# Batch 0's last transform stage moved into the end of the hand-ordered loop, with pools on both sides of SBUF

## The chip, the cores and the metric

The kernel runs on one NeuronCore of a Trainium2 chip. The metric is device time in microseconds (us). Three runs of the kernel before took 1730.43, 1730.86 and 1733.43 us; the median is 1730.86. A profile describes one more execution, instruction by instruction. Its engines are PE (TensorE's matmuls), PEld (TensorE's weight loads), ACT (ScalarE), DVE (VectorE), POOL (GpSimd) and SP (SyncE, which issues every DMA of this kernel; SPq in the rows).

## The reference

Two layers follow each other, on 8 batches of 3136 positions and 256 channels:

```python
X = np.fft.rfft(x, axis=1)
Yr = Xr @ w_r - Xi @ w_i + b_r
Yi = Xr @ w_i + Xi @ w_r + b_i
Yr = np.sign(Yr) * np.maximum(np.abs(Yr) - lam, 0.0)      # and Yi
y = np.fft.irfft(Yr + 1j * Yi, n=3136, axis=1)

h = np.maximum(y @ w_in, 0.0)                             # 256 -> 1024
conv_out = three-tap convolution of h along the positions, per channel
gate = 1.0 / (1.0 + np.exp(-conv_out))
out = (h * gate) @ w_out                                  # 1024 -> 256
```

So the first half is a spectral layer: a real Fourier transform along the positions, a complex 256 x 256 mix of the channels, a soft threshold, and the inverse transform. The second half is a gated feed-forward network (FFN).

## The kernel before

**Transforms as matmuls.** 3136 = 56 x 56, so each transform is two steps of small matmuls with tables of cosines and sines. Stage 1 (`stage1_pe`, L269) does the first step of the forward transform and stores its result in DRAM (`sc1`). Stage 2 (`stage2`, L312) does the second step, on a group of four frequencies `u`, and splits the result in a high and a low part. `mix` (L340) multiplies by the channel weights in three products of those parts. `shrink` (L349 to L355) is the soft threshold: two Relu on ScalarE into `r` and `q`, and a subtraction on GpSimd. Stage 3 (`stage3_pe`, L363) is the first step of the inverse transform; `stage3_out` copies its result to `z1` on ScalarE (L369) and stores it in DRAM (`sc2`) by two DMAs (L372, L378; four where the group is the first of a batch). Stage 4 (`stage4`, L495) is the last step: it loads `z2` from `sc2` (L489), multiplies by `i2`, and moves the result into `y`, which holds a whole batch in SBUF as a high part `yh` (ScalarE, L501) and a low part `yl` (VectorE, L502).

**The transform loop.** 8 batches of 7 groups make 56 items, `n_it = 56`. The loop at L427 runs 60 iterations and works as a pipeline: iteration `it` does stage 3 of item `it - 4`, stage 1 of an item further ahead, stage 2 of item `it`, `shrink` of item `it - 2`, `third` (the sum's high and low part) of item `it`, and `mix` of item `it - 1`. Stage 1 runs about ten items ahead, and is through by iteration 46. The last four iterations, 56 to 59, only drain the pipeline. In `background`, from iteration 3, VectorE prepares the FFN's weights in small steps between the others.

**What sets the order.** The loop stands in `with tc.manual_schedule()`. Inside it, each engine issues its instructions in the order in which the program text emits them, SyncE's DMAs too. Everything else is placed by a planner that goes by its own costs and by priorities, and it may put later instructions between those of the loop. Stage 4 of batch 0 stands behind the loop, with a raised priority (`HP = 500`), and so is placed by the planner. Stage 4 of the other batches is called from the FFN loop, three pieces per chunk, for the batch after the one in work.

**Stage 4 in pieces.** A batch has 28 values of `j`, in `NPC = 7` pieces of `JG = 4`. A piece loads one `z2` of 112 x 4 x 256 numbers (448 KB), does 8 matmul calls (16 in the profile) into one PSUM tile of two banks, and moves it out in two parts (three in piece 0), both channel halves together. `zio` holds three `z2` tiles.

**The FFN.** For each chunk of two times 448 positions and each of eight blocks of 128 hidden channels, `up` (L520) multiplies, applies Relu (L522), the three taps (L525 to L529), the sigmoid (L530) and the gate (L531), and splits the result (L534, L535); `down` (L548) multiplies by `w_out`, four blocks later. `y` is double: `y_a` for even and `y_b` for odd batches. The first `up` needs all of batch 0's `y`.

**Memory.** Every pool of the transform part is released when the loop ends (`ab`); the FFN's pools, `zio`, `y_a` and `y_b` among them, then take their place. A tile waits for those earlier tiles only whose bytes it takes.

Of the kernel before, what the change touches and what calls it, by code (L numbers as in the profile page):

```python
# [9 lines left out]
F32 = mybir.dt.float32  # L10
F32R = mybir.dt.float32r
I32 = mybir.dt.int32
AF = mybir.ActivationFunctionType
ALU = mybir.AluOpType
# [3 lines left out]
B, S, D, FF = 8, 3136, 256, 1024  # L18
R = 56
U = 28  # L20
SL = 57
SP = 64
H = 28
LAM = 0.01
UG = 4
NG = U // UG
JC = 4
P = 128
NT = D // P
NF = FF // P  # L30
CH = 448


def _tables():
# [90 lines left out]
def spectral_ffn_kernel(ctx: ExitStack, tc: tile.TileContext, x, w_r, w_i, b_r, b_i,  # L125
                        w_in, conv_w, w_out, fwd1, fwd2, inv1, inv2, out):
    nc = tc.nc
    K1, K2 = 2 * R, 2 * SP
# [3 lines left out]
    sc2 = [dram.tile([H, 4, U, D], F32, name=f"sc2_{b}") for b in range(B)]  # L132
# [4 lines left out]
    i2 = cst.tile([K1, 240], F32, name="i2")[:, 0:2 * K1].rearrange("p (a m) -> p a m", a=2)  # L137
# [4 lines left out]
    mlam, warm = small[:, 0:1], small[:, 1:2]  # L142


    with ExitStack() as ab:
        stg = ab.enter_context(tc.tile_pool(name="stg", bufs=1))
        wbp = ab.enter_context(tc.tile_pool(name="wbp", bufs=2))
        s1p = ab.enter_context(tc.tile_pool(name="s1p", bufs=2))
        c1 = ab.enter_context(tc.tile_pool(name="c1", bufs=1))
        a2p = ab.enter_context(tc.tile_pool(name="a2p", bufs=3))  # L150
        cmx = ab.enter_context(tc.tile_pool(name="cmx", bufs=1))
# [1 line left out]
        psx = ab.enter_context(tc.tile_pool(name="psx", bufs=6, space=PSUM))  # L153
        psa = ab.enter_context(tc.tile_pool(name="psa", bufs=1, space=PSUM))

        f1 = c1.tile([P, P], F32, name="f1")[:, 0:SP]
        t2 = c1.tile([K1, U, K2], F32, name="t2")
        bias = cmx.tile([P, 2, D], F32, name="bias")
        cmx.tile([P, 96], F32, name="pad")
# [161 lines left out]
        def third(xs):  # L321
            fh, fl, d = xs
            nc.scalar.copy(fh[:, :, 2], d)
            nc.gpsimd.tensor_tensor(fl[:, :, 2], d, fh[:, :, 2].bitcast(F32), op=ALU.subtract)  # L324
            return fh, fl

        def mix(xs):


            fh, fl = xs  # L330
            ps = {c: psx.tile([K2, UG // 2, D], F32, name=f"ps_mx{c}", tag="bank") for c in (2, 0, 1)}
            for c in (2, 0, 1):
                q = (1, 2, 0)[c]
                for k in range(UG // 2):
                    mm = []
                    for t in range(NT):
                        a = [f[:, t, c, 2 * k:2 * k + 2, :] for f in (fh, fl)]
                        mm += [(a[0], wmix_hi[:, t, q, :]), (a[0], wmix_lo[:, t, q, :]), (a[1], wmix_hi[:, t, q, :])]
                    for n, (lt, rh) in enumerate(mm):
                        nc.tensor.matmul(ps[c][:, k, :], lt, rh, start=(n == 0), stop=(n == len(mm) - 1))  # L340
            p1 = wk.tile([K2, 2, UG // 2, D], F32, name="p1")
            v = wk.tile([K2, 2, UG // 2, D], F32, name="v")
            for c in range(2):
                nc.vector.tensor_tensor(p1[:, c], ps[2], bias[:, c:c + 1, :].to_broadcast([K2, UG // 2, D]), op=ALU.add)
            for c in range(2):
                nc.vector.tensor_tensor(v[:, c], ps[c], p1[:, c], op=ALU.add)
            return v

        def shrink(v):  # L349
            r = wk.tile([K2, 2, UG // 2, D], F32, name="r", bufs=3)  # L350
            q = wk.tile([K2, 2, UG // 2, D], F32, name="q", bufs=1)
            nc.scalar.activation(r, v, AF.Relu, bias=mlam)
            nc.scalar.activation(q, v, AF.Relu, bias=mlam, scale=-1.0)  # L353
            nc.gpsimd.tensor_tensor(r, r, q, op=ALU.subtract)  # L354
            return r  # L355

        def stage3_pe(g, r):
# [28 lines left out]
        n_it = len(items)  # L386
        WP0, LAST = 3, n_it - 6
        a2s = {}
        p1 = NG
# [30 lines left out]
        def fetch(n):  # L420
            nonlocal nx
            while len(xq) < n and nx < n_it:
                xq.append(load_x(s1p, *items[nx], bufs=XRB)[0])
                nx += 1

        with tc.manual_schedule():
            for it in range(n_it + LAG):  # L427
                if it + 2 < n_it:
                    a2s[it + 2], _ = load_a2(*items[it + 2])
                if it < NG:  # L430
                    load_inv1(it)
                    if it + 1 < NG:
                        load_t2(it + 1)
                fetch(XRB)
                if it >= LAG:
                    g3 = items[it - LAG]
                    ps3 = stage3_pe(g3[1], ss.pop(it - LAG))
                if p1 < n_it:
                    ps1 = stage1_pe(xq.pop(0))
                if it >= LAG:  # L440
                    stage3_out(*g3, ps3)
                if WP0 <= it < n_it:
                    next(background, None)
                if p1 < n_it:
                    stage1_out(*items[p1], ps1)
                    p1 += 1
                if WP0 <= it < n_it:
                    for _ in range(2):
                        next(background, None)
                if it < n_it:  # L450
                    xs[it] = stage2(items[it][1], a2s.pop(it))
                if 0 <= it - 2 < n_it:
                    ss[it - 2] = shrink(vs.pop(it - 2))
                if it < n_it:
                    xs[it] = third(xs[it])
                if 0 <= it - 1 < n_it:
                    vs[it - 1] = mix(xs.pop(it - 1))
                if p1 < n_it and p1 < min(it + AHEAD, NG + 2 + it + it // 2):
                    fetch(1)
                    ps1 = stage1_pe(xq.pop(0))  # L460
                    stage1_out(*items[p1], ps1)
                    p1 += 1


    def pool(name, bufs=1, **kw):
        return ctx.enter_context(tc.tile_pool(name=name, bufs=bufs, reuse_waits="tile", **kw))

    zio, y_a = pool("zio", 3), pool("y_a")
    wk, hp, io, y_b = pool("cwk"), pool("chp", 3), pool("cio"), pool("y_b")
    wk.tile([P, 24], F32, name="pad", bufs=1)  # L470
    SW = 3168
    hp.tile([P, 8], F32, name="pad", bufs=1)
    psh, pso = pool("psh", 2, space=PSUM), pool("pso", space=PSUM)

    JG = 4
    NPC = H // JG

    def new_y(b):
        y = [(y_a, y_b)[b % 2].tile([P, NT, SW], F32R, name=nm) for nm in ("yh", "yl")]
        for q in y:  # L480
            qf = q.bitcast(F32)
            nc.vector.memset(qf[:, :, 0:1], 0.0)
            nc.vector.memset(qf[:, :, S + 1:S + 2], 0.0)
        return y

    def stage4(b, jg, y):

        z2 = zio.tile([K1, JG, D], F32, name="z2")
        nc.sync.dma_start(z2, sc2[b].rearrange("j q u e -> (q u) j e")[:, jg * JG:(jg + 1) * JG, :])  # L489
        ps = psh.tile([P, NT, 512], F32, name="ps_s4", tag="ps_h")  # L490
        psv = ps[:, :, 0:JG * K1].rearrange("p t (w m) -> p t w m", m=R)
        for t in range(NT):
            for j in range(JG):
                to = psv[:, t, j:2 * JG - j:2 * JG - 1 - 2 * j, :]
                nc.tensor.matmul(to, z2[:, j, t * P:(t + 1) * P], i2[:, 0 if jg or j else 1, :], start=(j == 0), stop=(j == JG - 1),  # L495
                                 skip_group_check=True)

        def move(w0, n, r0):
            src = psv[:, :, w0:w0 + n, :].rearrange("p t j m -> p t m j")
            hi, lo = [q[:, :, 1:S + 1].rearrange("p t (m r) -> p t m r", r=R)[:, :, :, r0:r0 + n] for q in y]  # L500
            nc.scalar.copy(hi, src)  # L501
            nc.vector.tensor_tensor(lo, src, hi.bitcast(F32), op=ALU.subtract)  # L502
        move(0, JG, jg * JG)
        if jg:
            move(JG, JG, R - jg * JG - JG + 1)
        else:
            move(JG, JG - 1, R - JG + 1)
            move(2 * JG - 1, 1, H)

    def up(f, halves):  # L510
        ps = psh.tile([P, 2, 512], F32, name="ps_h", tag="ps_h")
# [48 lines left out]

    LAG = 4
    TAP_DVE = (0, 4)
    HP = 500
    NH = S // CH
    NCH = B * NH // 2
    ys = {0: new_y(0)}
    for jg in range(NPC):
        with tc.high_priority(offset=HP):
            stage4(0, jg, ys[0])
    todo = []  # L570
    gs, accs = {}, None
    n_st = NCH * NF
    for st in range(n_st + LAG):
        if st < n_st:
            ci, f = divmod(st, NF)
            hv = [divmod(2 * ci + a, NH) for a in range(2)]
            if f == 0:
                nb = hv[1][0] + 1
                if nb < B and nb not in ys and hv[0][0] == hv[1][0]:
                    ys[nb] = new_y(nb)  # L580
                    todo = [(nb, jg) for jg in range(NPC)]
            gs[st] = up(f, [(ys[b], a * CH) for b, a in hv])
            if todo and f in (1, 4, 7):
                b, jg = todo.pop(0)
                stage4(b, jg, ys[b])
        if st >= LAG:
            ci, f = divmod(st - LAG, NF)
            accs = down(ci, f, gs.pop(st - LAG), accs)
# [24 lines left out]
```

## Time and profile before

| | |
|---|---|
| median of three runs | 1730.86 us (1730.43 to 1733.43) |
| the profiled execution | 1732.64 us, its span 1730.9 us, mean granted clock 0.986 |
| instructions | 30421 |
| PE busy | 1685.7 us (97%) |
| DVE busy | 1390.2 us (80%) |
| ACT busy | 1197.5 us (69%) |
| POOL busy | 209.9 us (12%) |
| end of the last `mix` | 505.3 us |
| first FFN matmul | 529.98 us |

The page divides the span into 40 slices of 43.3 us and gives the busy share of each engine in tenths. The windows view does the same for stretches one chooses: busy time and, in brackets, instructions of each engine, then the clock granted to TensorE (1.00 is full speed), the busy share of the DMA engines, and what they moved. The chain of waits follows the work that ended last back from the end. The timeline lists instructions in order of time, with the idle time before each and what ended it in square brackets. A matmul's length is that of one through the array, and neighbours overlap, so the distance of starts is what a matmul costs.

### The profile page before, as it was taken

The page shows a single profiled execution, that of the slowest core. Times are in us where ns is not written, and L with a number is a line of the kernel's source. Part 1 is how long each engine was busy: PE and PEld are TensorE (multiplying, and loading weights), DVE is VectorE, ACT ScalarE, POOL GpSimd, SP SyncE. Part 2 cuts the span into 40 slices and gives each one's busy share as a digit, 9 for nine tenths or more (in the row PEclk, how much of TensorE's full clock was granted, in tenths as well). Part 3 has the DMA queues.
Part 4 walks back from the last instruction along what each step waited for, and adds up shares of the span by engine and source line. Part 5 has one row for each costly group of instructions (what it writes and reads, how often), then busy time and mean ns, then how long its engine had stood idle before and what let it go on. Part 6 is the DMA issues. An engine that isn't in the chain of part 4 may idle for free.

```text
span 1730.9 us, 30421 instructions
## 1 busy us (share of the span) xinstructions
PE 1685.7 (97%) x12544; PEld 1556.3 (90%) x12544; DVE 1390.2 (80%) x1722; ACT 1197.5 (69%) x1589; POOL 209.9 (12%) x116
## 2 busy tenths in 40 slices
PE   4899999999998999999999999999999999999998
PEld 1688888888987999999999999999999999999998
DVE  2488888776546888888888888888888888888887
ACT  1477777677765777777777776776777677776776
POOL 0245445444440000000000000000000000000000
PEclk7899999999999999999999999999999999999999
DMA  8988888888432110111111011111101111100001
GB/s 222 250 259 244 235 248 248 217 225 237 139 101 72 54 43 23 43 54 44 43 54 44 22 43 55 43 43 55 43 22 47 51 43 44 43 22 23 22 22 43
DMA packets 115274, 163.77 MB, mean 95 GB/s; under 512 B 10680, under 2 KB 87728, under 8 KB 115136
## 3 DMA queue, kind: packets, MB, share of 16 engines
q1 hardware_dynamic: 115136, 161.83, 31.8%
q8 instruction: 99, 1.62, 0.4%
q14 instruction: 39, 0.32, 0.1%
HBM read 84.73 MB, written 77.07 MB: 93 GB/s over the span
## 4 chain that ended last, share of the span: by engine, by line
PE 95%; DMA 2%; DVE 1%; ACT 1%; issue 1%; SPq 1%; POOL 0%; ACTq 0%; DVEq 0%
PE acc L548 32%; PE ps_h L520 32%; PE ps_mx L340 14%; PE ps_s L312 7%; PE ps_s L495 6%; PE ps_s L363 3%; PE ps_s L269 3%; DMA xr<-in_x_dram 1%; DMA wm_raw<-in_w_i_dram 0%; SPq L274 0%; DVE yl L502 0%; ACT yh L501 0%; DMA sc<-ha 0%; DVE c L529 0%; DVE c L531 0%
## 5 line engine op out<-in xcount | busy, mean ns | idle before, releaser
L548 PE MATMUL acc<-wout,gh 128*128 128x256 f32 x3136 | 571.2, 281 | 0.0
L529 DVE SCALAR_TENSOR_TENSOR c<-h,cw,c 128x896 f32<-128x896 f32 x448 | 512.8, 1148 | 69.5 <-ACT c L527 66.5
L520 PE MATMUL ps_h<-yh,win 128*128 128x450 f32 x1792 | 550.3, 368 | 3.0 <-ACT yh L501 2.0
L548 PEld LDWEIGHTS acc<-wout,gh 128*128 128x128 f32 x3136 | 493.0, 188 | 6.1 <-ACT gh L534 0.3
L548 PE MATMUL acc<-wout,gl 128*128 128x256 f32 x1568 | 437.3, 280 | 0.4 <-DVE gl L535 0.4
L520 PEld LDWEIGHTS ps_h<-yh,win 128*128 128x128 f32 x1792 | 339.5, 189 | 29.3 <-ACT yh L501 2.2
L522 ACT ACTIVATE h<-ps_h 128x900 f32<-128x900 f32 x224 | 207.1, 924 | 197.5 <-PE ps_h L520 197.0
L520 PE MATMUL ps_h<-yl,win 128*128 128x450 f32 x896 | 329.8, 368 | 0.2 <-DVE yl L502 0.2
L548 PEld LDWEIGHTS acc<-wout,gl 128*128 128x128 f32 x1568 | 293.9, 188 | 1.2 <-DVE gl L535 0.6
L531 DVE TENSOR_TENSOR c<-h,c 128x896 f32<-128x896 f32 x224 | 243.7, 1088 | 40.9 <-ACT c L530 40.1
L535 DVE TENSOR_TENSOR gl<-c,gh 128x896 fp32r<-128x896 f32 x224 | 242.8, 1089 | 41.6 <-ACT gh L534 40.6
L534 ACT CAST gh<-c 128x896 fp32r<-128x896 f32 x224 | 210.7, 941 | 85.7 <-DVE c L531 85.7
L530 ACT ACTIVATE c<-c 128x896 f32<-128x896 f32 x224 | 212.5, 949 | 20.4 <-DVE c L529 18.3
L340 PE MATMUL ps_mx<-wmix_hi,fh 128*128 128x256 f32 x672 | 193.1, 287 | 0.0
L340 PE MATMUL ps_mx<-wmix_hi,fl 128*128 128x256 f32 x672 | 188.7, 281 | 1.7 <-POOL fl L324 1.7
L340 PE MATMUL ps_mx<-wmix_lo,fh 128*128 128x256 f32 x672 | 187.9, 280 | 0.0
L520 PEld LDWEIGHTS ps_h<-yl,win 128*128 128x128 f32 x896 | 169.4, 189 | 11.6 <-DVE yl L502 0.5
L527 ACT ACTIVATE c<-h,cw 128x896 f32<-128x896 f32 x168 | 175.9, 1047 | 1.8
L354 POOL TENSOR_TENSOR r<-r,q 128x1024 f32<-128x1024 f32 x56 | 133.5, 2384 | 235.8 <-ACT q L353 235.8
L312 PEld LDWEIGHTS ps_s<-t,a 112*128 112x128 f32 x896 | 106.8, 195 | 43.3 <-issue 39.2
L340 PEld LDWEIGHTS ps_mx<-wmix_hi,fl 128*128 128x128 f32 x672 | 126.6, 188 | 2.7 <-POOL fl L324 1.9
L340 PEld LDWEIGHTS ps_mx<-wmix_hi,fh 128*128 128x128 f32 x672 | 127.0, 189 | 0.4 <-issue 0.4
(77 smaller groups left out, 1715.1 us busy)
## 6 DMA issues: line engine op xcount, KB each, us to landing
xr<-in_x_dram SPq DMA_DIRECT2D x112, 224.0 KB
a<-sc SPq DMA_DIRECT2D x56, 448.0 KB
z<-sc SPq DMA_DIRECT2D x56, 448.0 KB
out_dram<-o SPq DMA_DIRECT2D x27, 896.0 KB
sc<-z SPq DMA_DIRECT2D x104, 224.0 KB
sc<-a SPq DMA_DIRECT2D x98, 224.0 KB
sc<-ha SPq DMA_DIRECT2D x14, 224.0 KB
win_bits<-in_moe_w_in_dram SPq DMA_DIRECT2D x4, 512.0 KB
```

What stands on the lines that cost most here:

```text
L312: nc.tensor.matmul(ps[:, k], a2[:, k, t * P:(t + 1) * P], t2[:, g * UG + k, :], start=(k == 0), stop=(k == UG - 1), skip_group_check=True)
L340: nc.tensor.matmul(ps[c][:, k, :], lt, rh, start=(n == 0), stop=(n == len(mm) - 1))
L354: nc.gpsimd.tensor_tensor(r, r, q, op=ALU.subtract)
L520: nc.tensor.matmul(ps[:, a, 0:CH + 2], lt, rh, start=(n == 0), stop=(n == len(mm) - 1))
L522: nc.scalar.activation(h, ps[:, :, 0:CH + 2], AF.Relu)
L527: nc.scalar.mul(c, h[:, :, 0:CH], cw[:, 0, f:f + 1])
L529: nc.vector.scalar_tensor_tensor(c, h[:, :, k:k + CH], cw[:, k, f:f + 1], c, op0=ALU.mult, op1=ALU.add)
L530: nc.scalar.activation(c, c, AF.Sigmoid)
L531: nc.vector.tensor_tensor(c, h[:, :, 1:CH + 1], c, op=ALU.mult)
L534: nc.scalar.copy(gh, c)
L535: nc.vector.tensor_tensor(gl, c, gh.bitcast(F32), op=ALU.subtract)
L548: nc.tensor.matmul(acc[m // 2][:, m % 2, :], lt[:, sl], rh[:, f, :], start=(f == 0 and n == 0 and m % 2 == 0), stop=(f == NF - 1 and n == ...
```

## The change

Stage 4 of batch 0 no longer stands behind the loop. Pieces 0 to 4 are emitted in iterations 48 to 52, between `third` and `mix`; pieces 5 and 6 in the drain, in iterations 57 and 58. There it takes its PSUM from the loop's own pool of six banks, one bank per channel half, and moves each half by itself. Stage 4 of the other batches keeps its form.

For that, `y_a` and `zio` have to exist before the loop ends. The pools of stage 1 and of the weights' preparation (`stg`, `wbp`, `s1p`, and `f1` in a pool of its own, `c0`) now stand at the other end of SBUF and are released at iteration 48; `zio` and `y_a` are opened in their place. Two tiles are saved: `mix` adds in place in `v` (before, in `p1`), and `shrink` writes its second Relu over `v` (before, into `q`). The weights' preparation has to end by iteration 48.

```diff
+SW = 3168
...
+    JG = 4
+    NPC = H // JG
+
+    def pool(name, bufs=1, **kw):
+        return ctx.enter_context(tc.tile_pool(name=name, bufs=bufs, reuse_waits="tile", **kw))
+
+    def new_y(yp):
+        y = [yp.tile([P, NT, SW], F32R, name=nm) for nm in ("yh", "yl")]
+        for q in y:
+            qf = q.bitcast(F32)
+            nc.vector.memset(qf[:, :, 0:1], 0.0)
+            nc.vector.memset(qf[:, :, S + 1:S + 2], 0.0)
+        return y
+
+    def stage4(b, jg, y, zio, parts):
+
+        z2 = zio.tile([K1, JG, D], F32, name="z2")
+        nc.sync.dma_start(z2, sc2[b].rearrange("j q u e -> (q u) j e")[:, jg * JG:(jg + 1) * JG, :])
+        for ts, ps in parts():
+            psv = ps[:, :, 0:JG * K1].rearrange("p t (w m) -> p t w m", m=R)
+            for n, t in enumerate(ts):
+                for j in range(JG):
+                    to = psv[:, n, j:2 * JG - j:2 * JG - 1 - 2 * j, :]
+                    nc.tensor.matmul(to, z2[:, j, t * P:(t + 1) * P], i2[:, 0 if jg or j else 1, :], start=(j == 0), stop=(j == JG - 1),
+                                     skip_group_check=True)
+
+            def move(w0, n, r0):
+                src = psv[:, :, w0:w0 + n, :].rearrange("p t j m -> p t m j")
+                hi, lo = [q[:, ts[0]:ts[-1] + 1, 1:S + 1].rearrange("p t (m r) -> p t m r", r=R)[:, :, :, r0:r0 + n] for q in y]
+                nc.scalar.copy(hi, src)
+                nc.vector.tensor_tensor(lo, src, hi.bitcast(F32), op=ALU.subtract)
...
+    pool("edge", side="right").tile([P, 48], F32, name="pad")
+
     with ExitStack() as ab:
-        stg = ab.enter_context(tc.tile_pool(name="stg", bufs=1))
-        wbp = ab.enter_context(tc.tile_pool(name="wbp", bufs=2))
-        s1p = ab.enter_context(tc.tile_pool(name="s1p", bufs=2))
+        eb = ExitStack()
+        stg = eb.enter_context(tc.tile_pool(name="stg", bufs=1, side="right"))
+        wbp = eb.enter_context(tc.tile_pool(name="wbp", bufs=2, side="right"))
+        s1p = eb.enter_context(tc.tile_pool(name="s1p", bufs=2, side="right"))
+        c0 = eb.enter_context(tc.tile_pool(name="c0", bufs=1, side="right"))
...
-            p1 = wk.tile([K2, 2, UG // 2, D], F32, name="p1")
             v = wk.tile([K2, 2, UG // 2, D], F32, name="v")
             for c in range(2):
-                nc.vector.tensor_tensor(p1[:, c], ps[2], bias[:, c:c + 1, :].to_broadcast([K2, UG // 2, D]), op=ALU.add)
+                nc.vector.tensor_tensor(v[:, c], ps[2], bias[:, c:c + 1, :].to_broadcast([K2, UG // 2, D]), op=ALU.add)
             for c in range(2):
-                nc.vector.tensor_tensor(v[:, c], ps[c], p1[:, c], op=ALU.add)
+                nc.vector.tensor_tensor(v[:, c], ps[c], v[:, c], op=ALU.add)
...
-            nc.scalar.activation(q, v, AF.Relu, bias=mlam, scale=-1.0)
-            nc.gpsimd.tensor_tensor(r, r, q, op=ALU.subtract)
+            nc.scalar.activation(v, v, AF.Relu, bias=mlam, scale=-1.0)
+            nc.gpsimd.tensor_tensor(r, r, v, op=ALU.subtract)
...
+        Y0, Y1 = n_it - NPC - 1, n_it - 3
+        jgs = iter(range(NPC))
+
+        def one_by_one():
+            for t in range(NT):
+                yield range(t, t + 1), psx.tile([P, 1, 512], F32, name="ps_s4", tag="bank")
+
...
-                if WP0 <= it < n_it:
+                if WP0 <= it < Y0:
                     next(background, None)
...
                 if it < n_it:
                     xs[it] = stage2(items[it][1], a2s.pop(it))
+                if it == Y0:
+                    eb.close()
+                    zio, y_a = pool("zio", 3, side="right"), pool("y_a", side="right")
+                    y0 = new_y(y_a)
                 if 0 <= it - 2 < n_it:
                     ss[it - 2] = shrink(vs.pop(it - 2))
                 if it < n_it:
                     xs[it] = third(xs[it])
+                if Y0 <= it < Y1 or n_it < it <= n_it + 2:
+                    stage4(0, next(jgs), y0, zio, one_by_one)
                 if 0 <= it - 1 < n_it:
                     vs[it - 1] = mix(xs.pop(it - 1))
...
-    zio, y_a = pool("zio", 3), pool("y_a")
...
+    def both():
+        yield range(NT), psh.tile([P, NT, 512], F32, name="ps_s4", tag="ps_h")
...
-    ys = {0: new_y(0)}
-    for jg in range(NPC):
-        with tc.high_priority(offset=HP):
-            stage4(0, jg, ys[0])
+    ys = {0: y0}
...
-                stage4(b, jg, ys[b])
+                stage4(b, jg, ys[b], zio, both)
```

More of the change, by code (lines that the diff above doesn't have):

```diff
@@ new lines, in stage4 @@
+    def stage4(b, jg, y, zio, parts):
[13 more added lines that the diff above has]
+                nc.vector.tensor_tensor(lo, src, hi.bitcast(F32), op=ALU.subtract)
+            move(0, JG, jg * JG)
+            if jg:
+                move(JG, JG, R - jg * JG - JG + 1)
+            else:
+                move(JG, JG - 1, R - JG + 1)
+                move(2 * JG - 1, 1, H)
@@ L154, in spectral_ffn_kernel @@
         psa = ab.enter_context(tc.tile_pool(name="psa", bufs=1, space=PSUM))
-        f1 = c1.tile([P, P], F32, name="f1")[:, 0:SP]
+        f1 = c0.tile([P, P], F32, name="f1")[:, 0:SP]
         t2 = c1.tile([K1, U, K2], F32, name="t2")
@@ L350, in shrink @@
             r = wk.tile([K2, 2, UG // 2, D], F32, name="r", bufs=3)
-            q = wk.tile([K2, 2, UG // 2, D], F32, name="q", bufs=1)
             nc.scalar.activation(r, v, AF.Relu, bias=mlam)
-            nc.scalar.activation(q, v, AF.Relu, bias=mlam, scale=-1.0)
-            nc.gpsimd.tensor_tensor(r, r, q, op=ALU.subtract)
+            nc.scalar.activation(v, v, AF.Relu, bias=mlam, scale=-1.0)
+            nc.gpsimd.tensor_tensor(r, r, v, op=ALU.subtract)
             return r
@@ L446, in spectral_ffn_kernel @@
                     p1 += 1
-                if WP0 <= it < n_it:
+                if WP0 <= it < Y0:
                     for _ in range(2):
@@ L462, in spectral_ffn_kernel @@
                     p1 += 1
-    def pool(name, bufs=1, **kw):
-        return ctx.enter_context(tc.tile_pool(name=name, bufs=bufs, reuse_waits="tile", **kw))
-    zio, y_a = pool("zio", 3), pool("y_a")
     wk, hp, io, y_b = pool("cwk"), pool("chp", 3), pool("cio"), pool("y_b")
     wk.tile([P, 24], F32, name="pad", bufs=1)
-    SW = 3168
     hp.tile([P, 8], F32, name="pad", bufs=1)
     psh, pso = pool("psh", 2, space=PSUM), pool("pso", space=PSUM)
[L475 to L508, printed above, removed]
+    def both():
+        yield range(NT), psh.tile([P, NT, 512], F32, name="ps_s4", tag="ps_h")
     def up(f, halves):
@@ L562, in spectral_ffn_kernel @@
     TAP_DVE = (0, 4)
-    HP = 500
     NH = S // CH
     NCH = B * NH // 2
-    ys = {0: new_y(0)}
-    for jg in range(NPC):
-        with tc.high_priority(offset=HP):
-            stage4(0, jg, ys[0])
+    ys = {0: y0}
     todo = []
@@ L579, in spectral_ffn_kernel @@
                 if nb < B and nb not in ys and hv[0][0] == hv[1][0]:
-                    ys[nb] = new_y(nb)
+                    ys[nb] = new_y((y_a, y_b)[nb % 2])
                     todo = [(nb, jg) for jg in range(NPC)]
```

## The prediction

> **What bounds the kernel now.** I read the stage table of the windows view first, then the chain of waits through the seam between the two halves of the kernel, then SyncE's queue and the transfers there. Columns of the windows view: window, its length, busy time and instruction count of PE, PEld, DVE, ACT and POOL, granted clock, DMA share, GB/s.
>
> ```profile
> 439.00:475.64 36.64, 36.64 (x341) 33.05 (x340) 21.36 (x41) 26.11 (x40) 17.54 (x11) 1.00 0.46 127
> 505.31:529.98 24.67, 18.09 (x162) 15.98 (x161) 8.99 (x20) 13.28 (x20) 2.37 (x1) 0.93 0.65 173
> 529.98:549.98 20.00, 18.41 (x97) 16.30 (x98) 14.33 (x17) 12.07 (x15) 0.00 (x0) 0.91 0.13 41
> ```
>
> The first row is iterations 48 to 52 of the transform loop, those that get a piece of the last stage: TensorE is busy for all 36.64 us, 7.33 us an iteration, and nothing else comes near it. The second row runs from the end of the last mix to the first FFN matmul: 24.67 us with 18.09 busy. The third is the FFN's first 20 us, 18.41 busy at a clock of 0.91. So the seam holds 6.6 + 1.6 us of idle TensorE and some slow clock. That is all the change can win.
>
> One iteration in the chain of waits (start, length, what), with ScalarE's copy of z1 and SyncE's issues beside it:
>
> ```profile
> 439.07 1.02 PE ps_s L363 x16
> 440.10 1.98 PE ps_s L312 x16
> 442.08 4.21 PE ps_mx L340 x36
> 446.29 1.02 PE ps_s L363 x16
> ...
> 440.16 1.01 ACT L369 COPY z<-ps_s 128x1024 f32<-128x1024 f32 x1 [1.58 <-PE ps_s L363]
> ...
> 441.20 0.31 SPq L372 DMA_DIRECT2D sc<-z  x1
> 441.56 0.38 SPq L378 DMA_DIRECT2D sc<-z  x1
> 442.11 0.53 SPq L302 DMA_DIRECT2D a<-sc  x1
> ```
>
> TensorE does stage 3 (L363), stage 2 (L312), mix (L340), with no gap. SyncE issues the two z1 stores only when ScalarE has copied stage 3's result, and the next load only behind them. That is the order of the program text, engine by engine, inside the hand-ordered loop.
>
> **The change, part by part.** *What is moved.* Seven pieces of batch 0's last stage leave the seam. Five go to iterations 48 to 52, between stage 2 and mix on TensorE; two go to iterations 57 and 58 of the drain. Each brings 16 matmuls, one 448 KB load on SyncE, and now four copies and four subtractions instead of two and two (three and three for piece 0).
>
> ```profile
> 551.54 1.77 PE ps_s L495 x16
> ...
> 506.40 3.55 PE ps_s L495 x30
> ...
> 382.82 0.37 SPq L489 DMA_DIRECT2D z<-sc  x1
> ```
>
> A piece costs TensorE 1.77 us wherever it stands. Before, the planner was free to place its load: the first went out at 382.82, over 120 us ahead of the first matmuls at 506.40. Now the load is written inside the iteration that uses it, behind the z1 stores of that iteration. By the rows above the second store is out at 441.56 + 0.38 = 441.94, so the load leaves at about 442.0. TensorE wants it at 442.08, when stage 2 ends. The load is issued as it is needed: **the change puts a whole transfer on the path of TensorE, five times in the loop and twice in the drain.**
>
> *What the load takes.* Before has the same pattern with the a2 load: as many bytes as a z2 load, behind the same two stores. It is issued at 442.11, and the transfers fade at 446 (last columns: DMA share, GB/s); the other rows are a z2 load alone and the first x load:
>
> ```profile
> a<-sc SPq DMA_DIRECT2D x56, 448.0 KB
> z<-sc SPq DMA_DIRECT2D x56, 448.0 KB
> ...
> 445.75:446.00 0.25, 0.25 (x4) 0.25 (x3) 0.25 (x2) 0.25 (x1) 0.25 (x1) 1.00 0.44 115
> 446.00:446.25 0.25, 0.25 (x7) 0.12 (x5) 0.25 (x1) 0.00 (x1) 0.25 (x1) 1.00 0.03 8
> ...
> 528.03 0.30 SPq L489 DMA_DIRECT2D z<-sc  x1
> 530.50:531.00 0.50, 0.36 (x1) 0.37 (x2) 0.08 (x1) 0.00 (x0) 0.00 (x0) 0.80 0.92 275
> 531.00:531.50 0.50, 0.50 (x3) 0.42 (x3) 0.00 (x0) 0.00 (x0) 0.00 (x0) 0.50 0.04 6
> ...
> 1.21 3.70 DMA xr<-in_x_dram
> 1.21:3.35 2.14, 0.00 (x0) 0.00 (x0) 0.00 (x0) 1.01 (x2) 0.00 (x0) 1.00 0.56 123
> ```
>
> Its last bytes pass 3.9 us after issue. A z2 load alone (528.03) needs 3.0 us: the lower end. What lies between the last byte and the matmul is seen only at the start: the first matmul is released 3.70 us after the first x load's issue (1.21), while 2.14 us x 123 GB/s = 263 KB, all of that load and the table ahead of it, have passed by 3.35. That leaves up to 4.91 - 3.35 = 1.6 us; but the second x load's bytes are among those counted, so the true tail is shorter. I take 0.8, between 0 and 1.6. The upper end adds 0.9 us, half of an a2 load's share, in case the a2 load now queued behind z2 competes with it. So z2 is usable at 442.0 + 3.9 + 0.8 = 446.7, and the stall is 446.7 - 442.08 = **4.6 us** (2.9 to 6.3).
>
> The Trainium skill, "DMA: Bandwidth & Descriptors", on the fixed cost of a transfer, puts some 2 us on every DMA and most of it behind the last byte, until the write is confirmed. By that the tail would be nearer 1.6 than 0.8 and the sum about 6 us higher; the x load's 3.70 us allows it and does not prove it.
>
> *Who waits behind it.* TensorE takes its work in order, so the 36 mix matmuls and all later iterations queue behind the piece. ScalarE's copies for the piece stand ahead of the next z1 copy and VectorE's subtractions ahead of mix's additions; both engines have room (26.11 and 21.36 of 36.64 us), and those operations end before mix does. With the loads early they would still fit: four 128x224 copies at some 0.46 us, between the two rows below, make 1.8 us more for ScalarE in an iteration then 9.1 us long.
>
> ```profile
> L501 ACT CAST yh<-ps_s 128x448 fp32r<-128x448 f32 x14 | 8.3, 608 | 10.2 <-DVE yl L502 5.2 <-PE ps_s L495 4.3 <-DVE yh L483 0.7
> L501 ACT CAST yh<-ps_s 128x112 fp32r<-128x112 f32 x2 | 0.8, 376 | 0.0
> ```
>
> *The clock.* Windows laid on the edges at which the granted clock changes:
>
> ```profile
> 510.32:513.73 3.41, 1.89 (x25) 1.37 (x18) 2.44 (x5) 3.05 (x6) 1.70 (x1) 1.00 0.83 233
> 520.55:523.96 3.41, 1.39 (x12) 1.42 (x13) 1.47 (x5) 0.58 (x1) 0.00 (x0) 1.00 0.99 236
> 523.96:527.37 3.41, 3.41 (x18) 3.41 (x17) 1.35 (x3) 1.20 (x2) 0.00 (x0) 0.50 0.48 124
> 527.37:530.78 3.41, 1.24 (x7) 0.78 (x7) 1.50 (x3) 1.19 (x2) 0.00 (x0) 1.00 0.54 168
> 530.78:534.19 3.41, 3.41 (x10) 3.02 (x11) 0.00 (x0) 0.00 (x0) 0.00 (x0) 0.50 0.05 11
> ...
> 522.57 5.42 PE L495 MATMUL ps_s<-i,z 112*128 112x112 f32 x32 [3.08 <-DVE yl L483]
> 529.98 0.47 PE L520 MATMUL ps_h<-yh,win 128*128 128x450 f32 x1 [1.98 <-ACT yh L501]
> ```
>
> A stretch of 3.41 us with 2.02 or 2.17 us idle is followed by one at half clock; one with 1.52 us idle is not. A stall of 4.6 us leaves at least 2.3 idle in one such stretch, so each is followed by 3.41 us at half clock, of which 2 to 3.4 fall on work and lose half of that. I take 1.5 us per stall (0 where the stall is 2.9 and splits evenly; 1.7 at most).
>
> The Trainium skill, "TensorE: Matmul & The Clock Gate", on how the clock gate oscillates in real kernels, warns of idle gaps over some 3.4 us, and of a loop that waits for a load in every tile and goes cold each time. Here idle stretches of 3.08 and 1.98 us already sufficed. At 4.6 us rule and rows agree; at 2.9 us the page's bound would spare the clock and the sum would be 5 x 1.5 lower.
>
> *The loop's sum.* An iteration becomes 3.01 (stages 3 and 2) + 4.6 + 1.77 + 4.21 + 1.5 = 15.1 us against 7.33: 7.8 more, **39 us over five**.
>
> *The drain.* Piece 5 is usable 7.6 us after its iteration's stage 3 begins, as in the loop (446.7 - 439.07). Then 1.77 + 1.02 (stage 3 of item 54) and 1.5 for the clock end at 11.9. Only then can z1 be copied and stored and piece 6's load go: 7.6 - 1.02 = 6.6 us on, at 18.5. Its matmuls (1.77 + 0.9 of slow clock) end at 21.2, the last half's two copies and two subtractions (4 x 0.46) at 23.0, where the FFN can begin; now it begins 24.67 after the same point. That gives back 1.7. TensorE has then been busy for 4 us, so the FFN starts at full clock and saves half of the cold 530.78:534.19, 1.6.
>
> *At nothing.* Writing q over v and p1 into v adds no wait: v's buffer is wanted again a whole iteration after GpSimd's subtraction has read it:
>
> ```profile
> 491.54 0.06 DVE L482 MEMSET yh<- 128x2 f32 x1
> ...
> 445.57 2.37 POOL L354 TENSOR_TENSOR r<-r,q 128x1024 f32<-128x1024 f32 x1 [3.82 <-ACT q L353]
> 452.02 1.28 DVE L344 TENSOR_TENSOR p<-ps_mx,bias 128x512 f32<-128x512 f32 x2
> ```
>
> That is 4.1 us between 447.94 and 452.02; without it VectorE would lose the difference, off TensorE's path. Pool sides, f1's place and y's memsets (four, 0.06 us each) cost nothing: those tiles' readers ended before iteration 48.
>
> **Sum:** 39 - 1.7 - 1.6 = +35.7 us, made against one profiled execution: its span is 1730.9, its time 1732.64, within the 1730.43 to 1733.43 of the runs, whose median is 1730.86. Added to the median: **1767 us** (1766.6).
>
> **Rivals.**
> *Short stall, clock kept* (2.9 us, no cold stretch): 5 x (2.9 + 1.77 - 0.12) = 22.8, where 0.12 is 7.33 less the 7.21 of TensorE's three stages, since mix would no longer start late. In the drain piece 5 is usable at 3.01 + 2.9 = 5.9, piece 6 at 5.9 + 2.79 + 4.9 = 13.6, the FFN begins at 13.6 + 1.77 + 1.84 = 17.2, 7.5 earlier; 1.6 more at the FFN. 22.8 - 7.5 - 1.6 = +13.7, 1745. For it: the lone load's 3.0 us. Against: the stores just ahead.
> *Long stall*: 5 x (6.3 + 1.77 + 1.7 - 0.12) = 48 in the loop, with nothing given back: 1779. For it: the x load's tail, and the a2 load behind.
> *Other side, loads early.* If the loads leave SyncE an iteration ahead, as the one at 382.82 did, no stall and no cold stretch arise. The loop grows by 5 x 1.77 = 8.9; the last stage 3 waits for GpSimd's subtraction,
>
> ```profile
> 505.38 1.02 PE ps_s L363 x16
> ...
> 509.64 2.37 POOL L354 TENSOR_TENSOR r<-r,q 128x1024 f32<-128x1024 f32 x1 [5.01 <-ACT q L353]
> ```
>
> which ends 512.01 - 505.31 = 6.7 us after the last mix; with its own 1.02 the FFN begins at about 8 instead of 24.67, and saves 1.6 of clock: 8.9 - 16.7 - 1.6 = -9.4, 1721. It decides wherever the load is out more than about 5 us before stage 2 ends. Against it: z1 stores and a2 loads keep their written order in every iteration.
> *Hidden anyway*: loop cost and seam gain cancel if the stall is about 1 us, within 0.2% of 1731. No row shows a load that short.
>
> **Chances.** Forecast 65% (1757 to 1777), short stall 11%, long stall 12%, early loads 8%, cancelled 4%. Differences under 0.2%, 3.5 us, can't be told from no change here. Faster 0.08, same 0.04, slower 0.88. The range of 1746 to 1781 leaves out the early loads, the cancelled case and the far ends of the stalls.
>
> **What would show it.** In the changed kernel: gaps of 4 to 5 us before the last stage's matmuls in five iterations, iterations of about 15 us, z loads issued right after L378's stores, half-clock stretches among them, and two gaps of 6 us in the drain. The forecast is wrong if z loads are issued an iteration before their matmuls, or TensorE runs through from 439 on.

## The result, and the profile after

The changed kernel took 1781.83 us (median of four runs, 1781.1 to 1782.08) beside 1731.89 us for the kernel before: a ratio of **1.0288** (95% interval 1.0274 to 1.0303), 50 us slower. I had forecast 1767 us and a range of 1746 to 1781, so the result lies just above the range. The direction and the place were right; the loss was some 40% larger than I had it (50 us instead of 36).

The windows view of the kernel after, for the stretches that answer to the three shown of before (iterations 48 to 52, the drain from the last mix to the first FFN matmul, the FFN's first 20 us); columns as there:

```profile
438.78:524.51 85.73, 58.64 (x425) 54.62 (x427) 31.48 (x67) 34.98 (x62) 20.82 (x12) 0.80 0.32 81
553.75:580.64 26.89, 12.31 (x82) 9.09 (x81) 3.87 (x9) 7.26 (x12) 2.34 (x1) 0.59 0.43 107
580.64:600.64 20.00, 18.61 (x104) 16.79 (x104) 15.14 (x21) 13.30 (x17) 0.00 (x0) 0.95 0.21 64
```

The five iterations take 85.73 us instead of 36.64, at a mean clock of 0.80. That is 49.1 us, nearly all of the loss. The drain, which I expected to shrink by 1.7 us, grew from 24.67 to 26.89.

One of the five in the chain of waits (start, length, what):

```profile
438.78 1.07 PE ps_s L404 x16
...
439.88 1.02 ACT z L410
...
440.91 0.31 SPq L413
...
441.27 0.38 SPq L419
...
441.70 5.62 DMA z<-sc
447.31 0.14 issue
447.45 3.73 PE ps_s L169 x16
451.18 4.99 PE ps_mx L383 x36
```

This is the chain that was forecast, link by link: stage 3, the copy of z1, the two stores, the load of z2, and only then the piece. TensorE's own row says what it waited for, and SyncE's rows (start, length, line) say what the load had ahead of it and behind it:

```profile
447.45 0.95 PE L169 MATMUL ps_s<-i,z 112*128 112x112 f32 x3 [5.66 <-DMA z<-sc]
```

```profile
441.27 0.38 SPq L419 DMA_DIRECT2D sc<-z  x1
441.70 0.64 SPq L163 DMA_DIRECT2D z<-sc  x1
442.38 0.88 SPq L345 DMA_DIRECT2D a<-sc  x1
```

The load leaves at 441.70, 2.92 us after stage 3 began, as forecast (2.93). The wait is 5.66 us here and 5.19 to 5.47 in the other four, where I had 4.6. Then the piece takes 3.73 us instead of 1.77 and mix 4.99 instead of 4.21. Windows of 3.41 us, laid within 0.3 us of the clock's edges, show why (TensorE's busy time is the second number, the clock stands before the last two; the half clock lasted from 445.92 to 452.75, hence 0.54 and 0.96 in two rows):

```profile
442.26:445.67 3.41, 0.00 (x0) 0.00 (x0) 1.99 (x8) 3.38 (x6) 0.00 (x0) 1.00 0.87 233
445.67:449.09 3.42, 1.64 (x8) 1.67 (x9) 0.00 (x0) 0.47 (x1) 3.38 (x2) 0.54 0.61 127
449.09:452.50 3.41, 3.41 (x18) 3.41 (x17) 1.41 (x4) 1.63 (x5) 0.19 (x1) 0.50 0.02 5
452.50:455.91 3.41, 3.41 (x30) 3.41 (x29) 2.52 (x5) 0.27 (x2) 0.00 (x0) 0.96 0.00 0
```

The first stretch is idle throughout, so the second is at half clock. TensorE is busy for 1.64 us of that one, and the third is at half clock too. Only the second and third together, two stretches, are followed by full clock. I had counted one.

### The profile page after: what moved, and what is told of

It reads as the page before. It is cut to its first block, busy times and chain, and to the rows that moved or that the text cites. A ratio compares the mean times of both kernels' runs of the same rounds, so it can differ in the third digit from the quotient of the medians.

```text
span 1780.3 us, 30459 instructions
## 1 busy us (share of the span) xinstructions
PE 1700.3 (96%) x12544; PEld 1569.7 (88%) x12544; DVE 1399.7 (79%) x1737; ACT 1206.6 (68%) x1604; POOL 209.5 (12%) x116
## 4 chain that ended last, share of the span: by engine, by line
PE 93%; DMA 4%; SPq 1%; DVE 1%; ACT 1%; issue 1%; POOL 0%; ACTq 0%; DVEq 0%; POOLq 0%
PE acc L564 31%; PE ps_h L536 31%; PE ps_mx L383 13%; PE ps_s L169 6%; PE ps_s L355 6%; PE ps_s L404 3%; PE ps_s L312 3%; DMA z<-sc 2%; DMA xr<-in_x_dram 1%; DMA wm_raw<-in_w_i_dram 0%; ACT z L410 0%; SPq L317 0%; DMA sc<-ha 0%; DVE c L545 0%; SPq L304 0%
## 5 line engine op out<-in xcount | busy, mean ns | idle before, releaser
L546 ACT ACTIVATE c<-c 128x896 f32<-128x896 f32 x224 | 212.4, 948 | 20.3 <-DVE c L545 18.3
L395 POOL TENSOR_TENSOR r<-r,v 128x1024 f32<-128x1024 f32 x56 | 133.0, 2374 | 285.5 <-ACT v L394 274.9
L169 PE MATMUL ps_s<-i,z 112*128 112x112 f32 x896 | 120.9, 293 | 41.7 <-DMA z<-sc 41.7
L169 PEld LDWEIGHTS ps_s<-i,z 112*128 112x128 f32 x896 | 117.5, 209 | 44.3 <-issue 43.7
```

Of the source, the lines that this page charges most:

```text
L546: nc.scalar.activation(c, c, AF.Sigmoid)
```

## The experiments

Four theories were in play: **late load** (each load of z2 leaves when it is needed, and TensorE waits for it), **the clock** (the waits cost half-clock stretches of their own), **crowding** (seven PSUM tiles for six banks, and eight moves more in an iteration), and **the memory** (other places for the pools, the threshold in place).

**The loads at the head of the iteration.** The piece stays where the change put it; its load moves ahead of the a2 load and the z1 stores of the same iteration.

```diff
             for it in range(n_it + LAG):
+                if it == Y0:
+                    eb.close()
+                    zio, y_a = pool("zio", 3, side="right"), pool("y_a", side="right")
+                    y0 = new_y(y_a)
+                z2 = None
+                if Y0 <= it < Y1 or n_it < it <= n_it + 2:
+                    jg4 = next(jgs)
+                    z2 = load_z2(0, jg4, zio)
...
-                    stage4(0, next(jgs), y0, zio, one_by_one)
+                    stage4(0, jg4, y0, zio, one_by_one, z2)
```

> Each of the seven loads of z2 is issued at the head of the iteration that uses it, ahead of the a2 load and the z1 stores; nothing else is changed but that the pools are swapped at the head of iteration 48. Late load (my theory): the gaps before the last stage's matmuls (5.2 to 5.7 us in the loop, 6.8 and 7.7 in the drain) and the half-clock stretches are gone, an iteration takes 7.21 + 1.77 = 9.0 us, the FFN begins about 8 us after the last mix, and the time is about 1721 us (1716 to 1728). Rival, crowding (seven PSUM tiles in six banks, four copies and four subtractions in the iteration): the iterations stay above 11 us and the time above 1740.

1730.03 us beside 1732.66 before: 0.9982 (0.9973 to 0.9991). Stretches of its windows view, the five iterations and the drain:

```profile
438.66:483.69 45.03, 45.03 (x424) 41.81 (x428) 27.61 (x64) 33.99 (x62) 20.33 (x12) 1.00 0.60 153
514.48:529.08 14.60, 9.66 (x82) 7.18 (x81) 3.77 (x9) 6.93 (x12) 2.35 (x1) 0.79 0.67 163
```

The loop does what late load said to the tenth: 9.0 us an iteration, TensorE never idle, full clock. Crowding falls, since everything that it names is still there. The time missed my 1721 mostly because of the drain (14.6 us instead of 8), where the chain of waits shows

```profile
516.96 0.39 SPq L422
517.35 0.04 issue
517.39 5.91 DMA z<-sc
523.30 0.14 issue
523.44 3.72 PE ps_s L172 x16
527.16 1.92 PE ps_s L407 x16
```

A drain iteration has no stage 2 and no mix. The head of one is therefore only stage 3 ahead of its piece, and behind the z1 stores of the one before it. Piece 6's load left at 517.39, TensorE was through with stage 3 by 518.50, and so the load was late again.

**All loads early.** The loads leave one per iteration from 48 on, so those of pieces 5 and 6 in iterations 53 and 54.

```diff
-                if Y0 <= it < Y1 or n_it < it <= n_it + 2:
-                    jg4 = next(jgs)
-                    z2 = load_z2(0, jg4, zio)
+                if Y0 <= it < Y0 + NPC:
+                    z2s.append(load_z2(0, it - Y0, zio))
```

> As the run with the loads at the head of the iteration, but the loads of pieces 5 and 6 leave in iterations 53 and 54, so that neither waits behind a z1 store of the drain. In that run piece 6 still waited some 5 us (518.4 to 523.44) and then ran at half clock (3.72 instead of 1.77, stage 3 1.92 instead of 1.02). Late load: both go, the FFN begins about 8 us after the last mix instead of 14.6, and the time is 6 to 7 us lower, about 1724. Rival, the drain waits for the chain through VectorE, ScalarE and GpSimd in any case: within 2 us of the 1730 of that run.

1725.41 us beside 1731.02: 0.9966 (0.9953 to 0.9978). The timeline of TensorE in the drain: no gap in front of the pieces (L172), one of 1.70 us for ScalarE in front of the last stage 3, and the first FFN matmul (L541) at 523.42, 8.7 us after the last mix.

```profile
515.65 2.04 PE L172 MATMUL ps_s<-i,z 112*128 112x112 f32 x16
517.61 1.09 PE L407 MATMUL ps_s<-r,i 64*64 64x256 f32 x16
518.64 2.04 PE L172 MATMUL ps_s<-i,z 112*128 112x112 f32 x16
522.38 1.09 PE L407 MATMUL ps_s<-r,i 64*64 64x256 f32 x16 [1.70 <-ACT z L413]
523.42 0.47 PE L541 MATMUL ps_h<-yh,win 128*128 128x450 f32 x1
```

The FFN begins 5.7 us earlier than in the run before (523.42 against 529.08). Against the kernel before, the ratio gains only 0.16%, some 3 us, where I expected 6 to 7. The chain of waits shows one thing that took the place of the late loads: VectorE's first step of the FFN (L546) stands behind the memsets of batch 1's y (L156), and these wait for z1's last store.

```profile
525.78 2.90 DMA sc<-z
...
528.80 0.06 DVE yl L156
528.86 0.67 DVE c L546
```

**Pieces 5 and 6 one iteration sooner**, in 56 and 57, otherwise the same:

```diff
-                if Y0 <= it < Y1 or n_it < it <= n_it + 2:
+                if Y0 <= it < Y1 or n_it <= it < n_it + 2:
```

> As the run with all loads early, but pieces 5 and 6 stand in iterations 56 and 57 instead of 57 and 58; piece 5 so comes ahead of the last mix, where TensorE waits 1.9 us for GpSimd, and that mix runs partly at half clock (5.79 instead of 4.2 us). Expected: 2 to 3.5 us below the run with all loads early, about 1721. If the mix's wait is only moved to the last stage 3 (which waits for the same GpSimd), the two are equal within 1 us.

**1723.04 us** beside 1731.02: 0.9947 (0.9934 to 0.996). It beats both kernels: 0.5% below the one before, 3.3% below the changed one. In the chain of waits of the run with all loads early, and of this one, the last mix:

```profile
508.90 5.79 PE ps_mx L386 x34
```

```profile
506.43 4.24 PE ps_mx L386 x34
```

Piece 5 fills the wait for GpSimd, and the mix runs at full clock, 1.55 us shorter in these two profiles. The medians are 2.4 us apart. The profiles can't divide that further, since the second shows an execution of 1719.51 us, the fastest of its five.

**Batch 1's first piece later.** On top of that version, batch 1's y is opened at the fourth block of the FFN's first chunk.

```diff
-            if f == 0:
-                nb = hv[1][0] + 1
-                if nb < B and nb not in ys and hv[0][0] == hv[1][0]:
+            nb = hv[1][0] + 1
+            if f == (0 if st >= NF else 3) and nb < B and nb not in ys and hv[0][0] == hv[1][0]:
```

> The fastest version so far (all loads early, pieces 5 and 6 in iterations 56 and 57), with batch 1's y opened and its first piece called at the fourth block of the first chunk instead of the first and second, so that neither its memsets, which wait for z1's last store, nor its piece stand in the FFN's first steps. If they cost there, 1 to 2 us less than 1723; if TensorE's queue is full either way, the same within 1 us.

1722.08 us beside 1731.54: 0.9948 (0.9933 to 0.9963), the same as without it. In the version that it is compared with, those memsets already stand behind VectorE's first four steps of the FFN (L546 at 522.06, the first memset at 527.18), so they hold nothing up there.

**The clock's own share.** Filling matmuls ahead of the piece, four and then six, keep TensorE busy while it waits.

```diff
+            for _ in range(fill if ts[0] == 0 else 0):
+                nc.tensor.matmul(ps[:, 0, :], t2[:, 0, :], t2[:, 0:4, :], start=True, stop=True, skip_group_check=True)
```

> The changed kernel, with four matmuls of 112 x 128 by 112 x 512 put on TensorE ahead of the last stage's in iterations 48 to 52; their result is overwritten. They should fill some 4 of the 5.4 us of waiting and leave the load as it is. If the clock takes a part of its own, the pieces run at full clock (1.77 instead of 3.73 us, mix 4.2 instead of 5.0), an iteration falls from 17.1 to about 14.4 us, and the time is about 13 us lower, 1768. If the load alone sets it, nothing changes: 1782. If the fill is longer than the wait, the iteration ends above 14.4.

> As the run with four filling matmuls, with six. With four, 3.6 of some 6 us were filled, the rest still brought half clock in three of five iterations (15.2, 16.6, 16.4, 16.7, 14.8 us). With six no idle over 1 us is left: all five iterations near 14.7 us if the clock is a term of its own, 12 us less than the changed kernel in the loop. If the load is slower the more TensorE works, iterations stay above 16.

With four: 1778.58 us beside 1732.66, 1.0258 (1.0238 to 1.0279); three of the five iterations still had half-clock stretches, so the first expectation (1768) was missed because the filling was too short. With six: 1770.99 us beside 1731.02, 1.0236 (1.0217 to 1.0254), some 10 us below the changed kernel. Its chain of waits, one of five like iterations:

```profile
440.10 5.69 DMA z<-sc
445.84 2.04 PE ps_s L171 x16
447.87 4.22 PE ps_mx L385 x36
```

The load is as late as ever, even 0.4 us later on average (5.7 against 5.3), but piece and mix run at full clock: 6.3 us instead of 3.73 + 4.99 = 8.7. The half clock is a term of its own, 2.4 us in each iteration, and it follows from the idle time, not from the piece. Net of the later load, an iteration falls from 17.15 to 15.15 us on average.

**What the load's length is made of.** Two runs change the bytes. The first halves the load itself; batch 0's output is then that of other data.

```diff
-        nc.sync.dma_start(z2, sc2[b].rearrange("j q u e -> (q u) j e")[:, jg * JG:(jg + 1) * JG, :])
+        nj = JG if b else JG // 2
+        nc.sync.dma_start(z2[:, 0:nj, :], sc2[b].rearrange("j q u e -> (q u) j e")[:, jg * JG:jg * JG + nj, :])
...
-                    nc.tensor.matmul(to, z2[:, j, t * P:(t + 1) * P],
+                    nc.tensor.matmul(to, z2[:, j % nj, t * P:(t + 1) * P],
```

> The changed kernel, but for batch 0 only two of a piece's four values of j are loaded (224 KB instead of 448 KB) and each is used twice, so the output of batch 0 is that of other data. If the wait is bytes at some 290 GB/s, it shortens by about 0.8 us in each of seven places, some 6 us in all (1776). If it is what lies around the bytes (issue, the stores ahead, the tail), it stays within 0.3 us and the time at 1782. A wait under 4 us in the loop would say that the load's own size was most of it.

The second leaves the load as large and puts the stores behind it, all but one row, which keeps the wait for z1 in place.

```diff
+            if later:
+                nc.sync.dma_start(dst[0, 0:1], z1[0:1])
+                return lambda: (nc.sync.dma_start(dst[0], z1[0:R]), nc.sync.dma_start(dst[1], z1[SP:SP + R]))
...
                     stage4(0, next(jgs), y0, zio, one_by_one)
+                    if rest:
+                        rest()
```

> The changed kernel, but in iterations 48 to 52 only one row of z1 (4 KB) is stored ahead of the load of z2 and all of z1 behind it, so the load leaves at the same place, with the same wait for z1, and has nearly nothing ahead of it. If bytes ahead of the load set its length, it falls from 5.2 to 5.7 us to the 3.0 us that a load alone took plus 0.7 to 1.0, about 4, and an iteration from 17.1 to 14.5 to 15.8. If the bytes behind it compete as much as those ahead, or the length is fixed, it stays above 5.

1769.91 us beside 1732.66, 1.0209 (1.0183 to 1.0235, two runs only), and 1769.36 us beside 1731.02, 1.0221 (1.0202 to 1.024). The load in the chain of waits, from its issue to its landing, in the first two of the five iterations, first with half the bytes, then with the stores behind:

```profile
441.21 3.69 DMA z<-sc
...
457.14 3.73 DMA z<-sc
```

```profile
440.60 3.70 DMA z<-sc
...
454.66 3.72 DMA z<-sc
```

Over the five iterations the load takes 3.64 to 3.94 us in the first run and 3.55 to 4.13 in the second, 3.77 on average in both. So both the bytes ahead (448 KB) and half its own (224 KB) take some 1.5 us off the 5.1 to 5.6 (5.3 on average) of the changed kernel. Half the bytes bought nearly twice the 0.8 us that I expected of them. With the stores and the a2 load both behind it, the load takes about what I estimate for one alone, 3.7 us: 3.0 to the last byte, as the lone load of before, and 0.6 to 0.7 from there to its landing, as in the drain (shown below). Piece 5 in the drain of the changed kernel has the stores ahead and no a2 load behind:

```profile
556.66 4.82 DMA z<-sc
```

That is 4.8, and in the three other runs that leave the drain as it is (four and six filling matmuls, the stores behind) the same load takes 4.65 to 4.82; the five in the loop, with the a2 load behind, average 5.3. So the load alone is about 3.7 us, the stores ahead bring it to 4.8, and the last 0.5 us is most likely the a2 load issued 0.7 us behind. No run changes that load by itself. Piece 6's load, with loads of batch 1 behind it, took 5.72, which fits; but with the stores and the a2 load 0.9 and 1.8 us behind it, the load hardly grew (3.77), so a transfer behind seems to count only if it follows closely.

**The memory alone.** The pools' places and the saved tiles stay; the seven pieces go back behind the loop, to the planner.

```diff
-                if Y0 <= it < Y1 or n_it < it <= n_it + 2:
-                    stage4(0, next(jgs), y0, zio, one_by_one)
...
+    for jg in range(NPC):
+        with tc.high_priority(offset=500):
+            stage4(0, jg, ys[0], zio, both)
```

> The pools' sides, the saved tiles and the early opening of y stay; the seven pieces go back behind the loop, where the planner places them and their loads. Late load: the time of the kernel before, 1731 us within 4. Rival, the memory's rearrangement costs (the threshold in place, other addresses): 1740 or more.

1734.59 us beside 1732.66: 1.0009 (0.9999 to 1.0018), no difference that this measurement tells. But its late iterations were longer than before's, so one part of it was tried by itself, the two in-place edits in the kernel before (the threshold's is shown; mix's addition in `v` instead of `p1` goes with it):

```diff
-            nc.scalar.activation(q, v, AF.Relu, bias=mlam, scale=-1.0)
-            nc.gpsimd.tensor_tensor(r, r, q, op=ALU.subtract)
+            nc.scalar.activation(v, v, AF.Relu, bias=mlam, scale=-1.0)
+            nc.gpsimd.tensor_tensor(r, r, v, op=ALU.subtract)
```

> The kernel before with one edit of the change alone: mix adds in place in v, and the threshold's second Relu is written over v. I had put it at nothing. In the run with the memory's rearrangement alone, the last iterations took 7.57 us where before they took 7.42, and the second Relu began 1.22 us after the first instead of 1.06. If writing over v is the cause, the late iterations of this run take 7.55 to 7.6 us too, eight of them 1 to 1.5 us more, which the time may just show (1732 to 1733 beside 1731). If they stay at 7.42, the cause is in the pools' places.

1735.74 us beside 1731.54: 1.0025 (1.0015 to 1.0034), some 4 us slower, more than expected. It is also more than the 0.09% of the run before, which holds the same two edits; why is open. ScalarE's two Relu of one iteration, in the kernel before and in this one:

```profile
487.78 1.19 ACT L352 ACTIVATE r<-v,small 128x1024 f32<-128x1024 f32 x1
488.84 1.17 ACT L353 ACTIVATE q<-v,small 128x1024 f32<-128x1024 f32 x1
```

```profile
488.99 1.18 ACT L350 ACTIVATE r<-v,small 128x1024 f32<-128x1024 f32 x1
490.21 1.16 ACT L351 ACTIVATE v<-v,small 128x1024 f32<-128x1024 f32 x1
```

Written over v, the second Relu starts 1.22 us after the first instead of 1.06, just after the first has ended (490.17) and no longer before: in these rows it waits until the first is done with v. The late iterations go round through ScalarE and GpSimd (the second Relu, GpSimd's subtraction, its part of `third`, ScalarE's next copy), and take 7.57 us instead of 7.42. That is about 1.5 us by the last mix. There the longer wait for GpSimd also tipped the clock: in this run

```profile
502.67 5.79 PE ps_mx L340 x34
```

takes 5.79 us where before it took 4.23. The two make 3.1 of the 4 us in this one profile. They weren't tried apart, and neither was mix's edit apart from the threshold's.

## Why the prediction was wrong, point by point

- *The load leaves as it is needed, seven times.* Right. It left 2.92 us after stage 3's start (forecast 2.93), and moving it ahead took the loop from 85.73 to 45.03 us.
- *"z2 is usable at 446.7, and the stall is 4.6 us."* Mis-sized: 5.42 on average. The bytes (3.9) and the tail (0.8) were nearly right, 4.8 where only the stores are ahead. The term left out of the middle, though it stood in the upper end, is most likely the a2 load close behind: 0.5 us, and 0.1 more passes from the landing to the matmul.
- *"I take 1.5 us per stall"* for the clock. This is the step that failed most: 2.7 us in the changed kernel (1.96 in the piece, 0.78 in mix). I let each wait cost one half-clock stretch and allowed 1.7 at most. But the wait reached into that stretch, which then had 1.64 us of work in 3.42, and a second followed. My rule came from before's rows, where every half-clock stretch in the seam was busy throughout.
- *"The loop's sum": 39 us over five.* 49.1, by these two terms: 5 x 0.8 + 5 x 1.2 = 10.
- *"The drain": 23.0 us.* 26.9. Piece 5's load was as late as said (usable 7.9 us after stage 3's start, forecast 7.6), piece 6's later (9.6), behind a stage 3 at half clock and with loads of batch 1 on its heels. And everything after the loads ran at half clock: the pieces 3.73 us, stage 3 1.96 and 1.92.
- *The FFN's start at full clock, 1.6 less.* Right in size only. The span gained 1.3 us from the FFN's start on, but the drain's half clock, from 558.56 on, lasted to 582.45, so the FFN's first 1.8 us still ran at half clock. The 10 us of the loop, 3.9 of the drain and 0.3 here make up the 14 us that the forecast was short.
- *"At nothing": writing q over v.* The buffer was free, as said, but I looked only for a wait on the buffer and not at the two ScalarE instructions that now read and write it one behind the other. In the kernel before, the two edits alone cost 0.25%. In the changed kernel their price isn't seen: the long iterations leave ScalarE and GpSimd time, and iterations 53 to 55 take 7.21 to 7.25 us.
- *Rivals.* The long stall (1779) came nearest, but by two errors that offset each other: its wait was too long (6.3) and its clock too short (1.7). The short stall had to keep the clock at a wait of 2.9 us; with the stores behind, waits of 3.06 to 3.65 us each brought half clock. The loads early, put at 1721, is what the repaired kernel does: 1725 with the pieces where the change put them, and 1723 with the last two moved.
- *A rule of the Trainium skill* ("DMA: Bandwidth & Descriptors", on the fixed cost of a transfer) would have put most of 2 us behind the last byte; the page works it out for transfers that GpSimd issues. These are issued by SyncE, and the drain's load of piece 5 shows what that takes: issued at 556.66, its bytes fade in the second row, and it lands at 561.48.

```profile
560.25:560.75 0.50, 0.00 (x0) 0.00 (x0) 0.00 (x0) 0.00 (x0) 0.31 (x1) 0.50 0.39 121
560.75:561.25 0.50, 0.00 (x0) 0.00 (x0) 0.00 (x0) 0.00 (x0) 0.00 (x0) 0.50 0.03 10
```

So some 0.6 us lie behind the last byte here, not most of 2.

## What to carry to other kernels

When work is moved into a loop whose order is written by hand, its loads move too, and a load that a planner had sent 100 us ahead may then leave at the moment it is needed: place the load first, and then the work. In short iterations, such as those of a drain, the head of the same iteration isn't early enough. A wait on TensorE costs itself and the half-clock work behind it, and the second can be half as large as the first.

## What the runs showed of the hardware that I had not expected

In the loop, a stretch at half clock that began with idle time was followed by another. In the changed kernel, 1.64 us busy of 3.42 did not end the half clock, and 3.41 of 3.41 did. The two runs that change the bytes have shorter waits, 3.06 to 4.23 us, and show where the line runs. In six of their ten iterations the piece began before the half-clock stretch did, and there was one such stretch; in the other four it began 0.1 to 0.9 us into it, and there were two. Here is one of each, with the stores behind; the pieces began at 458.51 and at 472.61, and from 462.26 the clock was full:

```profile
458.84:462.26 3.42, 3.42 (x19) 3.42 (x18) 0.79 (x2) 1.12 (x4) 3.22 (x2) 0.50 0.45 142
...
472.50:475.91 3.41, 3.30 (x15) 3.33 (x16) 0.40 (x1) 1.25 (x3) 3.34 (x2) 0.50 0.62 186
475.91:479.32 3.41, 3.41 (x18) 3.41 (x17) 1.55 (x4) 0.77 (x2) 0.24 (x1) 0.50 0.00 0
```

A stretch that is busy throughout isn't always the last, though. In the changed kernel's drain, where the stretch ahead had 0.35 us busy of 3.41, one was followed by another at half clock, and what sets it apart isn't shown:

```profile
561.97:565.39 3.42, 3.42 (x20) 3.22 (x23) 0.79 (x2) 0.76 (x3) 0.00 (x0) 0.50 0.00 0
565.39:568.80 3.41, 1.87 (x16) 0.68 (x16) 0.79 (x2) 1.76 (x3) 0.00 (x0) 0.50 0.00 0
```

In all five iterations of the changed kernel's loop the half clock began 6.8 to 7.1 us after stage 3 and lasted two stretches, some 6.8 us. It began every 17.07 us, which is five stretches, and the iterations took 17.0 to 17.4 us. Whether the clock's edges hold the loop in step or it only happened to fall there isn't shown; with the shorter waits, iterations ran from 13.9 to 16.2 us.

Two ScalarE instructions of which the second writes over what both read started 0.16 us further apart here than two that only read it (1.22 against 1.06), and the late iterations, which go round through them, were 0.15 us longer each.
